# A planned order of five engines: a port rule in the planner, products ahead of the first load, and shifted leads

## The chip, the cores and the metric

One core of a Trainium2 chip runs the whole program. The metric is the time of one execution on the device, in microseconds (us), lower being better. Five engines work side by side, each through its own queue in order: TensorE (PE, matrix products into PSUM), VectorE (DVE), ScalarE (ACT), GpSimd (POOL) and SyncE (SP, which issues the DMAs). TensorE's clock is granted at one of two levels, 1.2 and 2.4 GHz; the profile gives it as a share of the higher one.

## What is computed

Linear attention over 8 batches, 8 heads, 576 tokens and 64 columns a head, with an RMS norm, then two layers over the 4608 tokens.

```python
kv = einsum('bhsd,bhse->bhde', k, v)
out = einsum('bhsd,bhde->bhse', q, kv)
x = out / sqrt(mean(out * out, -1) + 1e-6) * g_norm      # 4608 tokens x 512

h = x @ w_in                                             # 512 -> 2048
x = (h * cos(h)) @ w_out                                 # 2048 -> 512

h = x @ w2_in                                            # 512 -> 1024
s = h * softmax(h)
x = (s - mean(s)) / sqrt(var(s) + 1e-6) * g_ln @ w2_out  # 1024 -> 512
```

## The kernel before

Every product is done in three (`mm3`, L184 to L187): both operands are held as a high and a low part of a fast type, and high x high, high x low and low x high are added up in PSUM. A **split** makes the parts: ScalarE casts the high part (L427), and VectorE or GpSimd subtracts it to give the low part (L428). Layer one has 2048 hidden columns; the first quarter of them is computed straight (**phase 0**), the other three by a scheme with seven products in place of eight on 2 x 2 blocks (**phase 1**, blocks of 3 or 4 pairs of tiles, `first_h` and `first_out`); layer two uses the scheme too (**phase 2**, 18 pairs of tiles).

*Phase 0* goes with the attention. Token blocks m = 0 to 8 of 512 tokens each have four steps c = 0 to 3. A step has a product of four groups of three (`step_h`) into bank ps0 or ps1, the cosine chain on it (`cosine`: ScalarE L775, VectorE L777, ScalarE L780, VectorE L784, ScalarE L786, VectorE L788), and a product of four groups (`step_out`) into ps2 to ps5, put after the next step's `step_h`. After the fourth step ScalarE copies ps2 to ps5 out (`block_out`, L823), and the next block's first product needs these banks. In between stand the attention's tiles: k and v products (L528) and their copies (L589, L549), the product with q (L596, L646), a square (L600, L655), a reduction (L602, L657), GpSimd's power (L572, L573), a norm (L607, L673), a transposition (L612, L678) and the split of the result (L616, L618, L755, L757). The last block's four halves are taken from SBUF in `pair_prep` (four L427, then four L428). The weights come as 64-bit floats: a conversion is one ScalarE step (L399) and five others (L401, L403, L406, L408 on VectorE, L410 on VectorE at the start and on GpSimd later); jobs that convert the weights of the later phases run beside the steps of phase 0.

*Phase 1* begins with `prep_first`: a pair of tiles is loaded from DRAM, GpSimd makes four sums (L716), and four splits give the operands `rxa` and `rxb`.

The order of all instructions is written by a planner, `Flow.run`, before the program is built. Each operation is a task with an engine, a duration, its reads and writes, and a number `at`. The planner gives the engine that can start first its next task: among the tasks that can start by then, the one with the lowest `at`. So durations and `at` decide the order, and the engines then run it as far as data allow. A task with `port` is one of VectorE or GpSimd on SBUF. Where two such overlapped, the later one was lengthened by a share `PORT` of the overlap:

```python
a, b = port.get("DVE" if eng == "POOL" else "POOL", (0.0, 0.0))
t.end += PORT * max(0.0, min(b, t.end) - max(a, s))
```

Of the kernel before, what the change touches and what calls it, by code (L numbers as in the profile page):

```python
# [1393 lines left out]
```

## Time and profile before

| | |
|---|---|
| time of the kernel, median of 3 runs | 1261.39 us (1260.58 to 1262.4) |
| the profiled execution | 1262.73 us |
| its span, first to last instruction | 1260.9 us |
| busy: TensorE / VectorE / ScalarE / GpSimd | 1228.7 / 970.1 / 728.5 / 739.3 us |
| share of the span | 97% / 77% / 58% / 59% |
| share of the critical chain on TensorE | 91% |
| mean granted TensorE clock | 0.995 |

Matmuls are pipelined: a busy TensorE is not one at its peak, and the product shows as longer (0.39 us) than the distance from one to the next. An idle time in brackets is that of the engine just before the instruction, with what ended it. Tile names are the program's without numbers: `ps` is a PSUM bank, `rg` and `rx` hold operands, `fconv`, `pa` and `ws` belong to the conversions, `att` to the attention.

### The profile page before, as it was taken

Reading aid. Unit: us, or ns where it says so; the run is one execution under the profiler, and the core shown is the slowest. Engines: PE = TensorE matmul, PEld = TensorE weight load, DVE = VectorE, ACT = ScalarE, POOL = GpSimd, SP = SyncE. Lnnn points to the kernel's source line nnn. Section 1 sums busy time; section 2 is a strip of 40 time slices with the busy share of each in tenths; the row PEclk is TensorE's granted clock in tenths of the full one; section 3 lists DMA queues with packets and bytes.
Section 4 is the critical chain, followed back from the end, with each engine's and each line's share of the span. In section 5 each row is a group of like instructions: output and inputs, shape, how many; then the busy total and the mean of one; then the engine's idle time right before and its main releaser. Section 6 shows DMA issues by size and latency. Waiting matters only on the chain.

```text
span 1260.9 us, 20503 instructions
## 1 busy us (share of the span) xinstructions
PE 1228.7 (97%) x7224; PEld 1078.9 (86%) x7224; DVE 970.1 (77%) x1537; ACT 728.5 (58%) x1366; POOL 739.3 (59%) x686
## 2 busy tenths in 40 slices
PE   6899999988999999999999999999999999999998
PEld 4788887876999999888888888888898999898997
DVE  7977787887887887979685846654887888887875
ACT  5767666665663663656364625442666566666653
POOL 2355666666566667665773524262776667686732
PEclk9999999998999999999999999999999999999999
DMA  9799898686967958773866374499112121111000
GB/s 329 262 309 317 288 316 307 207 267 220 297 215 227 303 205 254 247 250 105 282 198 208 100 216 129 132 307 285 59 37 65 35 67 35 60 43 59 18 34 35
DMA packets 188009, 231.01 MB, mean 183 GB/s; under 512 B 11777, under 2 KB 123393, under 8 KB 187905
## 3 DMA queue, kind: packets, MB, share of 16 engines
q1 hardware_dynamic: 187904, 229.69, 56.0%
q8 instruction: 57, 0.93, 0.3%
q14 instruction: 48, 0.39, 0.1%
HBM read 159.91 MB, written 69.73 MB: 182 GB/s over the span
## 4 chain that ended last, share of the span: by engine, by line
PE 91%; DVE 5%; ACT 2%; issue 1%; DMA 0%; POOL 0%; DVEq 0%; ACTq 0%
PE ps L185 28%; PE ps L187 28%; PE ps L186 28%; PE ps L1043 2%; PE ps L646 2%; PE ps L528 2%; PE ps L678 1%; DVE fconv L403 0%; DVE rxb L428 0%; DVE fconv L401 0%; DMA fconv<-w 0%; DVE fconv L406 0%; DVE rxa L428 0%; ACT xf L684 0%; DVE fconv L408 0%
## 5 line engine op out<-in xcount | busy, mean ns | idle before, releaser
L185 PE MATMUL ps<-rg,rwo 128*128 128x512 f32 (+2 forms) x912 | 316.9, 347 | 5.5 <-ACT fh L823 4.1
L187 PE MATMUL ps<-rg,rwo 128*128 128x512 f32 (+2 forms) x912 | 314.0, 344 | 0.0
L186 PE MATMUL ps<-rg,rwo 128*128 128x512 f32 (+2 forms) x912 | 313.8, 344 | 0.0
L791 POOL TENSOR_TENSOR rg<-fh,rg 128x512 fp32r<-128x512 f32 (+1 forms) x120 | 151.5, 1274 | 160.1 <-ACT rg L786 153.2
L185 PEld LDWEIGHTS ps<-rg,rwo 128*128 128x128 f32 x912 | 172.4, 189 | 24.6 <-ACT fh L823 4.5
L186 PEld LDWEIGHTS ps<-rg,rwo 128*128 128x128 f32 x912 | 172.5, 189 | 17.8
L187 PEld LDWEIGHTS ps<-rg,rwo 128*128 128x128 f32 x912 | 172.2, 189 | 17.2
L185 PE MATMUL ps<-rxa,rwi 128*128 128x512 f32 (+1 forms) x384 | 146.7, 382 | 0.4 <-DVE fh L872 0.4
L186 PE MATMUL ps<-rxa,rwi 128*128 128x512 f32 (+1 forms) x384 | 144.5, 376 | 0.0
L187 PE MATMUL ps<-rxa,rwi 128*128 128x512 f32 (+1 forms) x384 | 144.3, 376 | 0.0
L775 ACT ACTIVATE fh<-ps 128x512 int32<-128x512 f32 (+1 forms) x126 | 71.5, 568 | 103.7 <-PE ps L187 92.1
L780 ACT ACTIVATE fh<-fh,const 128x512 f32<-128x512 f32 (+1 forms) x156 | 106.5, 692 | 36.3 <-DVE fh L777 35.5
L428 POOL TENSOR_TENSOR ws<-fconv,ws 128x512 fp32r<-128x512 f32 x68 | 87.4, 1288 | 42.3 <-ACT ws L427 27.1
L185 PE MATMUL ps<-rxb,rwi 128*128 128x512 f32 (+1 forms) x288 | 109.8, 381 | 0.0
L186 PE MATMUL ps<-rxb,rwi 128*128 128x512 f32 (+1 forms) x288 | 108.5, 377 | 0.0
L187 PE MATMUL ps<-rxb,rwi 128*128 128x512 f32 (+1 forms) x288 | 108.2, 376 | 0.0
L777 DVE SCALAR_TENSOR_TENSOR fh<-ps,fh 128x512 f32<-128x512 f32 (+1 forms) x126 | 80.9, 647 | 31.9 <-ACT fh L775 30.5
L923 DVE TENSOR_TENSOR mid<-ps,mid 128x512 f32<-128x512 f32 (+1 forms) x90 | 57.0, 634 | 60.0 <-PE ps L187 59.6
L410 POOL TENSOR_TENSOR fconv<-fconv 128x512 f32<-128x512 f32 x40 | 52.3, 1308 | 61.7 <-DVE fconv L408 61.7
L428 POOL TENSOR_TENSOR rwi<-sf,rwi 128x512 fp32r<-128x512 f32 x36 | 49.1, 1364 | 67.0 <-ACT rwi L427 66.9
L786 ACT CAST rg<-fh 128x512 fp32r<-128x512 f32 (+1 forms) x120 | 68.1, 577 | 29.7 <-DVE fh L784 28.4
L185 PEld LDWEIGHTS ps<-rxa,rwi 128*128 128x128 f32 x384 | 72.2, 188 | 11.4 <-DVE fh L872 0.7
(154 smaller groups left out, 2971.5 us busy)
## 6 DMA issues: line engine op xcount, KB each, us to landing
rwi<-wid SPq DMA_DIRECT2D x66, 512.0 KB, 5.1
rwo<-wod SPq DMA_DIRECT2D x88, 256.0 KB, 4.0
att<-qkv SPq DMA_DIRECT2D x32, 512.0 KB, 6.6
fconv<-w SPq DMA_DIRECT2D x28, 512.0 KB, 5.1
px<-fh SPq DMA_DIRECT2D x42, 256.0 KB, 4.4
xd<-xf SPq DMA_DIRECT2D x18, 512.0 KB, 4.4
wid<-ws SPq DMA_DIRECT2D x18, 512.0 KB, 3.9
xf<-xd SPq DMA_DIRECT2D x18, 512.0 KB, 4.9
```

The lines of the kernel that those rows point to most:

```text
L185: PE.matmul(ps, lhsT=lh, rhs=rh, start=start, stop=False, skip_group_check=more)
L186: PE.matmul(ps, lhsT=lh, rhs=rl, start=False, stop=False, skip_group_check=more)
L187: PE.matmul(ps, lhsT=ll, rhs=rh, start=False, stop=stop, skip_group_check=more)
L410: either(on_dve, 512, lambda eng: eng.tensor_tensor(out=buf[wk], in0=buf[yk], in1=buf[wk], op=ALU.add), r=[yk, wk], w=[wk], at=at)
L428: either(on_dve, n, lambda eng: eng.tensor_tensor(out=lo(), in0=src(), in1=f(hi()), op=ALU.subtract), [*keys, *hk], lk, at)
L528: PE.matmul(buf[bk][e * D:(e + 1) * D, p % 2 * D:(p % 2 + 1) * D], lhsT=k_[:, at_:at_ + D], rhs=k_[:, v_ + at_:v_ + at_ + D], start=(c == ...
L775: add("ACT", e_(0.6, 0.385, n), lambda: ACT.activation(out=tt().bitcast(I32), in_=h(), func=AF.Copy, scale=INV_2PI, bias=0.25), r=r, w=[tk ...
L777: add("DVE", e_(0.69, 0.418, n), lambda: DVE.scalar_tensor_tensor(out=tt(), in0=h(), scalar=INV_2PI, in1=tt().bitcast(I32), op0=ALU.mult, ...
L780: add("ACT", e_(0.725, 0.509, n), lambda: ACT.activation(out=tt(), in_=tt(), func=AF.Sin, bias=buf["halfpi"][:, 0:1], scale=TWO_PI), r=[tk ...
L786: add("ACT", e_(0.62, 0.405, n), lambda: ACT.copy(out=hi(), in_=g()), r=gk, w=hk, at=t + 2)
L791: either(on_dve, n, lambda eng: eng.tensor_tensor(out=lo(), in0=g(), in1=f(hi()), op=ALU.subtract), [*gk, *hk], lk, t + 2)
L923: add("DVE", e_(0.69, 0.418, n), lambda ak=ak, bk=bk: DVE.tensor_tensor(out=buf[ak][:, 0:n], in0=buf[bk][:, 0:n], in1=buf[ak][:, 0:n], op= ...
```

## The change

1. **The planner's port rule.** The lengthening by `PORT` is gone. A task with `port` now starts no sooner than the end of the other engine's last such task, less `LEAD` = 0.14 us. Three small operations of layer two (L1010, L1018) no longer count as `port`. `SLACK` of VectorE and GpSimd goes from 1.11 and 1.1 to 1.04.
2. **Products of the identity.** `N_WARM` = 15 products of the 128x128 identity with itself, into ps0, stand first on TensorE. Nothing reads them.
3. **Low parts of the first block of phase 1.** `prep_first` gives the fourth split (256 columns) of the first block's three pairs to GpSimd; before, all were VectorE's.
4. **Leads.** `at` values of jobs, loads, attention slots and of the softmax are shifted. `JOBS_LATE` and `COS_LEAD` are 0, `PAIR_DVE` is 2 and `FIRST_LEAD` 30, which changes nothing.

```diff
-E2_LEAD, SOFT_AT, SOFT_D, Q_OFF, CP_D = 15.86, 9.73, 0.94, 4.97, 10
+E2_LEAD, SOFT_AT, SOFT_D, Q_OFF, CP_D = 15.86, 10.63, -0.65, 4.97, 10
-PREP_LEAD, PREP_D, H_LATE, H_EARLY, JOB_AT = 4.22, 4, 0.41, 0.09, 8.99
+PREP_LEAD, PREP_D, H_LATE, H_EARLY, JOB_AT = 4.22, 4, 0.31, -0.01, 8.99
-SLOTS0, SLOT_T, SLOT_D, ... = 2, -7.89, 0.78, ...
+SLOTS0, SLOT_T, SLOT_D, ... = 2, -8.17, 0.14, ...
-CV_AHEAD, W_LOAD = 14.87, (-26.91, -24.38, -8.84, 7.59, 19.93, 10.16, 24.12, 28.58)
+CV_AHEAD, W_LOAD = 14.87, (-21.63, -23.98, -8.29, 7.59, 19.93, 10.16, 24.81, 28.58)
+N_WARM, JOBS_LATE, LATE_AT, LATE_D, FIRST_LEAD, COS_LEAD, FIRST_DVE, PAIR_DVE = 15, 0, 2.31, 9, 30, 0, 3, 2
-GAP, PE_LAT, PORT = 0.04, 0.18, 0.58
-SLACK = {"DVE": 1.11, "ACT": 1.1, "POOL": 1.1}
+GAP, PE_LAT, LEAD = 0.04, 0.18, 0.14
+SLACK = {"DVE": 1.04, "ACT": 1.1, "POOL": 1.04}
-ATT_LEAD, CV_LEAD, Q_LEAD, PRI = 8, 7.69, 16, 20
+ATT_LEAD, CV_LEAD, Q_LEAD, PRI = 7.15, 7.69, 16, 22.66
...
         def start(t):
-            return max(self.free.get(t.eng, 0.0), t.ready)
+            s = max(self.free.get(t.eng, 0.0), t.ready)
+            return max(s, locked["DVE" if t.eng == "POOL" else "POOL"] - LEAD) if t.port else s
...
             if t.port:
-                a, b = port.get("DVE" if eng == "POOL" else "POOL", (0.0, 0.0))
-                t.end += PORT * max(0.0, min(b, t.end) - max(a, s))
-                port[eng] = s, t.end
+                locked[eng] = t.end
...
+    for _ in range(N_WARM):
+        add("PE", 0.222, lambda: PE.matmul(buf[BANKS[0]][:, 0:P], lhsT=buf["ident"], rhs=buf["ident"], start=True,
+                                           stop=True), r=["ident"], w=[BANKS[0]], at=-50)
...
-    prep_first(item["t0"] // 2 + j, j, at - (PREP_LEAD if n else 30) + PREP_D * j, lambda i: True)
+    prep_first(item["t0"] // 2 + j, j, at - (PREP_LEAD if n else FIRST_LEAD) + PREP_D * j, lambda i: n or i < FIRST_DVE)
```

The engines' instructions are the same ones but for these; their order changes nearly everywhere. On TensorE, the last transposition of the attention (L678) stood nine groups of three ahead of the first product of the last block, and now stands 18 ahead; counted from the start, the last attention tiles come up to 13 groups earlier.

ScalarE at the start, before (`fconv` and `pa` hold two weight chunks in conversion, `rg_4` and `rg_5` are their high parts, `att_17` is the block of k-v products):

```order
L399 ACTIVATE fconv_0_101<-fconv_0_101 128x512
L399 ACTIVATE pa_8_127<-fconv_0_101 128x512
L427 CAST rg_4_89<-fconv_0_101 128x512
L589 COPY att_17_152<-ps2_0_175 64x64 x4
L600 ACTIVATE fh_0_115<-ps4_0_183 128x512
L427 CAST rg_5_90<-fconv_0_101 128x512
```
and in the new order:

```order
L399 ACTIVATE pa_8_127<-fconv_0_101 128x512
L399 ACTIVATE fconv_0_101<-fconv_0_101 128x512
L589 COPY att_17_152<-ps2_0_175 64x64 x2
L427 CAST rg_4_89<-fconv_0_101 128x512
L589 COPY att_17_152<-ps2_0_175 64x64 x2
L427 CAST rg_5_90<-fconv_0_101 128x512
L600 ACTIVATE fh_0_115<-ps4_0_183 128x512
```
The first product's copy now goes ahead of the first cast, and both casts ahead of the first square (L600).

VectorE in the change from phase 0 to phase 1 (`rxa`, `rxb` are operands of phase 1, `ps0` and `ps1` hold the steps of the last block), before:

```order
L428 TENSOR_TENSOR rxb_0_2588<-xf_0_110,rxb_0_2588 128x2x128
L401 TENSOR_SCALAR fconv_0_101<-fconv_0_101 128x512
L403 SCALAR_TENSOR_TENSOR fconv_0_101<-fconv_0_101 128x512
L428 TENSOR_TENSOR rxb_0_2588<-xf_1_111,rxb_0_2588 128x4x128
L428 TENSOR_TENSOR rxb_0_2588<-xf_1_111,rxb_0_2588 128x2x128
L777 SCALAR_TENSOR_TENSOR fh_0_115<-ps1_0_171,fh_0_115 128x512
L777 SCALAR_TENSOR_TENSOR fh_0_115<-ps0_0_167,fh_0_115 128x512
L784 TENSOR_TENSOR ps1_0_171<-ps1_0_171,fh_0_115 128x512
L784 TENSOR_TENSOR ps0_0_167<-ps0_0_167,fh_0_115 128x512
L788 TENSOR_TENSOR rg_1_86<-ps1_0_171,rg_1_86 128x512
L788 TENSOR_TENSOR rg_0_85<-ps0_0_167,rg_0_85 128x512
```
and in the new order:

```order
L401 TENSOR_SCALAR fconv_0_101<-fconv_0_101 128x512
L403 SCALAR_TENSOR_TENSOR fconv_0_101<-fconv_0_101 128x512
L777 SCALAR_TENSOR_TENSOR fh_0_115<-ps1_0_171,fh_0_115 128x512
L406 TENSOR_SCALAR fconv_0_101<-fconv_0_101 128x512
L784 TENSOR_TENSOR ps1_0_171<-ps1_0_171,fh_0_115 128x512
L408 SCALAR_TENSOR_TENSOR fconv_0_101<-fconv_0_101 128x512
L788 TENSOR_TENSOR rg_1_86<-ps1_0_171,rg_1_86 128x512
L428 TENSOR_TENSOR rxa_1_81<-sf_0_105,rxa_1_81 128x4x128
L777 SCALAR_TENSOR_TENSOR fh_0_115<-ps0_0_167,fh_0_115 128x512
L428 TENSOR_TENSOR rxb_0_2541<-xf_1_111,rxb_0_2541 128x4x128
L784 TENSOR_TENSOR ps0_0_167<-ps0_0_167,fh_0_115 128x512
```
The two L777, which stood one behind the other behind a conversion and two splits, stand apart, each soon followed by its own L784.

ScalarE in the same place, before (`ps2` to `ps5` are the banks that `block_out` empties):

```order
L823 COPY fh_0_115<-ps4_0_183 128x512
L399 ACTIVATE fconv_0_101<-fconv_0_101 128x512
L427 CAST rxb_0_2588<-xf_1_111 128x4x128
L427 CAST rxb_0_2588<-xf_1_111 128x2x128
L427 CAST ws_1_97<-fconv_0_101 128x512
L775 ACTIVATE fh_0_115<-ps0_0_167 128x512
L427 CAST ws_0_96<-fconv_0_101 128x512
L780 ACTIVATE fh_0_115<-fh_0_115,const_1_67 128x512
L823 COPY fh_0_115<-ps5_0_187 128x512
L780 ACTIVATE fh_0_115<-fh_0_115,const_1_67 128x512
```
and in the new order:

```order
L775 ACTIVATE fh_0_115<-ps1_0_171 128x512
L427 CAST rxa_0_80<-sf_1_106 128x4x128
L823 COPY fh_0_115<-ps2_0_175 128x512
L780 ACTIVATE fh_0_115<-fh_0_115,const_1_67 128x512
L823 COPY fh_0_115<-ps3_0_179 128x512
L823 COPY fh_0_115<-ps4_0_183 128x512
L786 CAST rg_1_86<-ps1_0_171 128x512
L427 CAST rxa_1_81<-sf_1_106 128x4x128
L775 ACTIVATE fh_0_115<-ps0_0_167 128x512
L780 ACTIVATE fh_0_115<-fh_0_115,const_1_67 128x512
L399 ACTIVATE fconv_0_101<-fconv_0_101 128x512
L823 COPY fh_0_115<-ps5_0_187 128x512
```
The copy of `ps5` had a conversion step (L399), four casts, one L775 and one L780 between it and that of `ps4`; now it has one L786, one cast, one L775, one L780 and one L399. Some 10 us earlier, where the last block's halves are split, the four casts stood behind all four copies of the block before, and stand now ahead of three of them.

## Rows read from the trace of the kernel before

**Rows 1.** Busy us (instructions) per stretch: PE, PEld, DVE, ACT, POOL; clock; DMA; GB/s.

```profile
0.00:60.00 60.00, 44.41 (x429) 36.02 (x430) 48.82 (x88) 36.11 (x73) 17.61 (x22) 1.00 0.88 291
60.00:260.00 200.00, 198.08 (x1368) 164.40 (x1367) 153.66 (x237) 135.43 (x251) 127.44 (x120) 1.00 0.86 288
260.00:320.00 60.00, 51.27 (x221) 41.90 (x220) 49.44 (x64) 35.18 (x65) 39.75 (x37) 0.91 0.80 254
320.00:1240.00 920.00, 919.57 (x5096) 822.58 (x5095) 709.13 (x1134) 515.38 (x967) 548.39 (x503) 1.00 0.47 152
...
sum 1261.00, PE 1228.66 PEld 1078.91 DVE 970.10 ACT 728.54 POOL 739.33; mean PE 245.73 PEld 215.78 DVE 194.02 ACT 145.71 POOL 147.87
```

**Rows 2.** Timeline of TensorE at the start: start us, us, engine, line, tiles, [idle before].

```profile
7.59 1.34 PE L528 MATMUL ps<-att 128*64 128x64 f32 x20 [7.59 <-DMA att<-qkv]
...
10.76 2.08 PE L596 MATMUL ps<-att,att 128*128 128x128 f32 x8
...
13.82 1.16 PE L596 MATMUL ps<-att,att 128*128 128x128 f32 x8
14.91 0.80 PE L528 MATMUL ps<-att 128*64 128x64 f32 x20
```

**Rows 3.** Timeline of the other engines at the start.

```profile
1.00 0.29 POOL masks.py:199 TENSOR_SCALAR_AFFINE_SELECT const<-const 128x128 f32<-128x128 f32 x1
...
5.36 0.43 DVE L401 TENSOR_SCALAR fconv<-fconv 128x512 uint32<-128x512 uint32 x1 [2.11 <-ACT fconv L399]
...
11.19 0.69 DVE L410 TENSOR_TENSOR fconv<-pa,fconv 128x512 f32<-128x512 f32 x1
...
12.87 0.60 ACT L600 ACTIVATE fh<-ps 128x512 f32<-128x512 f32 x1 [1.58 <-PE ps L596]
```

**Rows 4.** Waits of TensorE from 265 to 320: us, times, longest.

```profile
PE ps L185 <- ACT fh L823: 4.1, 1, 4.1
PE ps L185 <- DVE rg L788: 3.1, 2, 2.1
PE ps L186 <- DVE rg L428: 1.2, 1, 1.2
PE ps L185 <- DVE fh L872: 0.4, 1, 0.4
```

**Rows 5.** Timeline about the split of the last block's halves.

```profile
264.78 1.29 POOL L410 TENSOR_TENSOR fconv<-fconv 128x512 f32<-128x512 f32 x1
...
266.79 0.60 PE L678 MATMUL ps<-const,att 128*128 128x128 f32 x4
...
268.02 2.17 ACT L427 CAST rg<-xf 128x512 fp32r<-128x512 f32 x4
...
270.22 4.67 DVE L428 TENSOR_TENSOR rg<-xf,rg 128x512 fp32r<-128x512 f32 x4
...
270.38 1.67 POOL L410 TENSOR_TENSOR fconv<-fconv 128x512 f32<-128x512 f32 x1 [2.28 <-DVE fconv L408]
...
272.78 1.56 POOL L428 TENSOR_TENSOR ws<-fconv,ws 128x512 fp32r<-128x512 f32 x1 [0.73 <-ACT ws L427]
```

**Rows 6.** Busy us per stretch, as in rows 1, in the change of phases.

```profile
290.00:295.00 5.00, 1.88 (x9) 1.23 (x7) 5.00 (x5) 1.30 (x3) 4.90 (x5) 1.00 0.28 106
...
300.00:305.00 5.00, 5.00 (x16) 3.92 (x15) 0.91 (x2) 1.29 (x3) 0.49 (x1) 0.63 0.72 233
305.00:310.00 5.00, 5.00 (x23) 4.13 (x22) 4.02 (x7) 3.27 (x7) 3.33 (x4) 1.00 0.82 256
```

**Rows 7.** Timeline of VectorE and ScalarE in the change of phases.

```profile
289.90 1.67 DVE L403 SCALAR_TENSOR_TENSOR fconv<-fconv 128x512 uint32<-128x512 uint32 x1
...
291.49 2.62 DVE L428 TENSOR_TENSOR rxb<-xf,rxb 128x512 fp32r<-128x512 f32 x2
...
294.74 0.72 ACT L780 ACTIVATE fh<-fh,const 128x512 f32<-128x512 f32 x1 [3.70 <-DVE fh L777]
...
304.70 0.68 DVE L428 TENSOR_TENSOR rxa<-sf,rxa 128x512 fp32r<-128x512 f32 x1
```

More of the change, by code (lines that the diff above doesn't have):

```diff
@@ L48 @@
 BLOCKS = (0, 3), (6, 3), (12, 4), (20, 4), (28, 4)
-E2_LEAD, SOFT_AT, SOFT_D, Q_OFF, CP_D = 15.86, 9.73, 0.94, 4.97, 10
+E2_LEAD, SOFT_AT, SOFT_D, Q_OFF, CP_D = 15.86, 10.63, -0.65, 4.97, 10
 E2_JOBS = (0, 0, 0, 0, 0, 0, 1, 2, 0, 1, 2, 0, 1, 1, 0)
-PREP_LEAD, PREP_D, H_LATE, H_EARLY, JOB_AT = 4.22, 4, 0.41, 0.09, 8.99
+PREP_LEAD, PREP_D, H_LATE, H_EARLY, JOB_AT = 4.22, 4, 0.31, -0.01, 8.99
 T0, STEP_A, ITEM = 25, 8.14, 44.22
-SLOTS0, SLOT_T, SLOT_D, SLOT_LATE, SLOT_RATE, JOB0, JOB1 = 2, -7.89, 0.78, -10.82, 2.42, 5, 32
-CV_AHEAD, W_LOAD = 14.87, (-26.91, -24.38, -8.84, 7.59, 19.93, 10.16, 24.12, 28.58)
+SLOTS0, SLOT_T, SLOT_D, SLOT_LATE, SLOT_RATE, JOB0, JOB1 = 2, -8.17, 0.14, -10.82, 2.42, 5, 32
+CV_AHEAD, W_LOAD = 14.87, (-21.63, -23.98, -8.29, 7.59, 19.93, 10.16, 24.81, 28.58)
 MM4, MM2 = 0.68, 0.355
-GAP, PE_LAT, PORT = 0.04, 0.18, 0.58
-SLACK = {"DVE": 1.11, "ACT": 1.1, "POOL": 1.1}
-DMA_ISSUE, DMA_START, DMA_END, DMA_AHEAD = 0.5, 2.29, 1.84, 4
+N_WARM, JOBS_LATE, LATE_AT, LATE_D, FIRST_LEAD, COS_LEAD, FIRST_DVE, PAIR_DVE = 15, 0, 2.31, 9, 30, 0, 3, 2
+GAP, PE_LAT, LEAD = 0.04, 0.18, 0.14
+SLACK = {"DVE": 1.04, "ACT": 1.1, "POOL": 1.04}
+DMA_ISSUE, DMA_START, DMA_END, DMA_AHEAD = 0.5, 2.1, 1.84, 4
 OVER = {"DVE": 0.084, "ACT": 0.104, "POOL": 0.042}
 XPRI = 10
-ATT_LEAD, CV_LEAD, Q_LEAD, PRI = 8, 7.69, 16, 20
-KV_T = 0.59
-PAIR_C, TR_LAG, OUT_LAG = 21.19, 19.02, 29.5
+ATT_LEAD, CV_LEAD, Q_LEAD, PRI = 7.15, 7.69, 16, 22.66
+KV_T = 0.64
+PAIR_C, TR_LAG, OUT_LAG = 20.75, 19.02, 29.5
 SMALL = ("nmx", "z", "sp", "nmp", "v", "zz", "ry")
@@ L126, in run @@
     def run(self):
-        ready, port, served = {}, {}, 0.0
+        ready, locked, served = {}, {"DVE": -1e3, "POOL": -1e3}, 0.0
         def release(t):
@@ L767, in pair_prep @@
                   lambda col=col: xo(m, 0)[:, :, col], lambda col=col: xo(m, 1)[:, :, col],
-                  [("xhk", i, j, h)], [("xlk", i, j, h)], at, True)
+                  [("xhk", i, j, h)], [("xlk", i, j, h)], at, h < PAIR_DVE)
     def cosine(h, psrc, tk, n, hi, lo, r, hk, lk, t, on_dve, there=False):
@@ L806, in step_h @@
         cosine(lambda: buf[hb], True, tts(), 512, lambda: rg(j)[:, 0, :], lambda: rg(j)[:, 1, :],
-               [hb], [("gs", j)], [("gsl", j)], at, True, True)
+               [hb], [("gs", j)], [("gsl", j)], at - COS_LEAD, True, True)
     def step_out(c, j, at):
@@ L1010, in soft @@
         add("DVE", 1.216, lambda: DVE.tensor_reduce(out=sm("nmx"), in_=buf[hk], axis=AX.X, op=ALU.max, negate=True),
-            r=[*halves], w=[("nmx", n)], at=at)
+            r=[*halves], w=[("nmx", n)], at=at, ps=True)
         add("ACT", 1.24, lambda: ACT.activation(out=buf[ek], in_=buf[hk], func=AF.Exp, bias=sm("nmx")[:, 0:1],
@@ L1018, in soft @@
         add("DVE", 0.15, lambda: DVE.tensor_scalar(out=sm("nmp"), in0=sm("sp"), scalar1=-1.0 / FP, scalar2=None,
-                                                  op0=ALU.mult), r=[("sp", n)], w=[("nmp", n)], at=at)
+                                                  op0=ALU.mult), r=[("sp", n)], w=[("nmp", n)], at=at, ps=True)
         add("ACT", 0.2, lambda: ACT.activation(out=sm("zz"), in_=sm("z"), func=AF.Square, scale=1e-3,
@@ L1225, in tile_kernel @@
     jobs = [x for fp in range(2, NFP) for x in (job_in(fp), job_out(fp, 0), job_out(fp, 1))]
+    late, jobs = jobs[len(jobs) - JOBS_LATE:], jobs[:len(jobs) - JOBS_LATE]
     n_jobs = len(jobs)
@@ L1278, in half_out @@
             first_out(item, half, at, dur / KC)
+    for i, job in enumerate(late):
+        job(T1_ + LATE_AT + LATE_D * i)
     prev = None
```

## The prediction

> **What bounds the kernel now.** I read the busy time by stretch first [rows 1]. TensorE is busy 1228.66 of 1261 us, so the order of the other engines can matter only where TensorE stands still. In the 920 us from 320 to 1240 it stands still 0.43 us, in the 200 us from 60 to 260 1.92 us: nothing is to be had there. It stands still 15.59 us in the first 60 us (7.59 of them before the first product, whose k and v have not landed [rows 2]), 8.73 us from 260 to 320, and what is left, 5.67 us, at the end. Then I read the waits of the 60 us about the change of layers [rows 4]: 4.1 + 3.1 + 1.2 + 0.4 = 8.8 us, all of TensorE, for ScalarE's copies (L823) and for VectorE. Idle time there is paid twice: from 300 to 305 the granted clock is 0.63 (that is the 1.2 GHz level for most of it), and 5 us hold 16 products in place of 23 [rows 6]. At 5/23 = 0.22 us each (0.65 a group of three) that is 7 x 0.22 = 1.5 us lost. There is a second such stretch after the 3.1 us for L788; with the parts on either side I put both at 3.5 us. So the change of layers costs 8.8 + 3.5 = 12.3 us, the start 8.0 beyond the landing of k.
>
> Why VectorE is late there: it is busy for all of the 5 us from 290 to 295, in which TensorE does 1.88 us [rows 6]. Four L428 take 4.67 us [rows 5]; one takes 0.68 where GpSimd is idle [rows 7], so 4 x 0.68 = 2.72 would do. GpSimd's own two instructions took 1.67 and 1.56 us in that time, against 1.29 before it [rows 5]. Later an L403 takes 1.67 and two L428 take 2.62 [rows 7]. **That is the collision the new planner lays out for**, and in the old order one such pile (L403, two L428) stands ahead of two L777. L780 waits 3.70 us for L777 [rows 7], L823 stands behind L780, and TensorE's product waits 4.1 us for the bank that L823 empties [rows 4].
>
> The Trainium skill bears on this, in "SBUF — State Buffer", Who interferes with whom: a VectorE instruction with two SBUF inputs and a GpSimd instruction that reads SBUF take one port in turn, and the later one blocks wholly. The trace agrees only nearly: alone the six instructions of [rows 5] come to 2.72 + 2.58 = 5.30 us, and they were done in 4.67.
>
> **The change, part by part. (1) The start.** Fifteen products of the identity run before k lands. Four 128x128 products show as eight passes [rows 2], so fifteen are 30; at 2.08/8 = 0.26 to 1.16/8 = 0.145 us each they take 4.4 to 7.8 us. The identity is written at 1.29 [rows 3], so they end between 5.7 and 9.1 and cost between nothing and 1.5 us of the first k pair at 7.59. I take nothing: in the trace the passes went from 0.26 to 0.145 us some 6 us after TensorE's first work, and here that should fall inside the 30. What they give: the first two k-v groups and the first q group go from 1.34, 1.34 and 2.08 to 0.80, 0.80 and 1.16 [rows 2], 2.0 us of TensorE. Little of it reaches the path, since the new ScalarE order puts both weight casts (L427) ahead of the first L600, and the second of them needs ten VectorE conversion steps. These ran from 5.36 to 11.19 + 0.69 = 11.88, with one L428 among them that is now behind them, so they end near 11.3 [rows 3]. A copy and a cast then bring L600 to about 12.2 against 12.87 [rows 3]: 0.7 us. On VectorE the third norm (L607) has one reduction (L602) less ahead of it: another 0.6. A little more (0.2) for smaller moves makes 1.5 us; ends 0 and 4 us (half of the 8.0).
>
> **(2) The change of layers.** What goes. The products on the last block's first tiles waited 1.2 us for the splits L428 of its halves. The last transposition (L678) began at 266.79 and the last split ended at 270.22 + 4.67 = 274.89 [rows 5]: 8.1 us. The old order gives nine groups of three to fill them (5.9 us), the new one 18 (11.7 us): gone. The 3.1 us for L788: the old order has L777 behind the four splits and L784 behind four conversion steps, the new one has L777 and L784 of that step ahead of the splits: gone. The 4.1 us: in the new order the L777 that the L780 ahead of the last bank's copy waits for has one L428 straight ahead of it, where it had a conversion and two L428: gone. With the waits the half clock goes, 3.5 us. What comes. (a) On ScalarE the four casts (2.17 us [rows 5]) now stand ahead of three of the four bank copies of the block before. From the last L678 to the end of the third copy are L678, the copy out of its bank, four casts, and five more of 0.54 to 0.72 (the four casts' share, and L780 [rows 7]): 0.6 + 0.7 + 2.2 + 3.0 = 6.5, while TensorE has eight groups (5.2 us) to do. That is a new wait of 1.3; ends 0.5 (starts overlap) and 2.7 (the cast between them waits for one GpSimd instruction of 1.29). I take 1.5. (b) VectorE. Between the first split of the last block and the split of the third tile of layer one there are 41 instructions in the new order, 34 of 0.69 and seven of 0.43 (L401, L406) [rows 3]: 26.5 us. TensorE covers them with 54 groups (35.1 us) less some 3.5 until the first split: 31.6. That leaves 5.1 us for collisions. The stretched instructions of [rows 5, 7] cost 4.67 - 2.72, 1.67 - 0.69 and 2.62 - 1.36, together 4.2 us, in 9 us of some 30 of VectorE's work; the rest is less dense, and I put the whole at 7.5. With as many TensorE waits 2.4, and with a third fewer nothing; three splits of 256 columns move from VectorE to GpSimd, which lengthens GpSimd's share. I take 2.5, ends 0 and 8. Sum: -12.3 + 1.5 + 2.5 = -8.3.
>
> By the skill's rule of turns alone, GpSimd's work in that stretch (nine of 1.29 and 19 half as wide) and VectorE's 18 two-input instructions could not lie side by side: 11.6 + 12.3 + 12.4 = 36.3 against 35.1, so 1.2 us more of waiting would come, and 1253.8 in place of the time below.
>
> **(3) What pays for it.** The last attention tiles come earlier, the last by 13 groups (8.5 us), into a stretch where VectorE and ScalarE already work; TensorE waits there 1.9 us in 200 [rows 1]. I take +1.0, ends 0 (DMA and engines have room: VectorE 153.7, ScalarE 135.4 of 200) and +6.
>
> **(4) The rest.** Layer one after 320 and the whole of layer two: TensorE has 0.43 us to lose or gain; the reordering hides behind it. If a new order let it wait as in 60 to 260 it would cost 0.4 to 3; I take 0. The end: TensorE's last 120 instructions stand in the same order; the last L1092 and L1012 swap, which is 0.4 us either way. I take 0.
>
> Sum: -1.5 - 8.3 + 1.0 = **-8.8 us**. The profiled execution took 1262.73 us, 1.83 over its span of 1260.9, and lies 1.34 above the median; so 1253.9 for it, and **1252.6** against the median of 1261.39.
>
> **Rivals.** A, *no change*: VectorE stays the bound of the change of layers. It does the same instructions but three, collisions come to their 7.5 us wherever they stand, a wait for L788 or L823 forms again and the clock falls again. For it: VectorE is busy 49.44 of 60 us there [rows 1]. Against it: the longest wait was one pile ahead of one L777, and the new order has none. Then (2) is -2 and the time 1259.4 or more, up to 1263.
>
> B, *slower*: the attention tiles that were pulled forward. Each half tile needs a reduction, GpSimd's power, a norm, a transposition and a split in turn, and all of these now share VectorE with steps that TensorE waits for. The nearest row is the wait for L823, 4.1 us [rows 4]. Two such waits and a half-clock stretch after each (1.5 to 2) come to 12 us and more than eat the 9.8 us won elsewhere; the case turns slower from 12.3 us of new waits on. 1264 to 1268.
>
> C, *the identity's products do not carry*: they end early, the clock falls again before k lands, and the start keeps its rates. The trace has the pattern (TensorE does 1.88 of the 5 us from 290, and soon after the granted clock is 0.63 [rows 6]). That takes 0.7 from (1): 1253.3, inside the forecast's range. The Trainium skill has the rule behind it in "TensorE: Matmul & The Clock Gate", Part 1: the slow state is the default, activity lifts it, idleness brings it back; the trace's 2.08 and then 1.16 us for the same eight passes agree.
>
> **How the numbers follow.** Changes of this kernel within 0.2% (2.5 us) can't be told from none. The forecast (with C) has 0.76, A 0.13, B 0.11. The range takes the forecast's own spread, from -14 (start 4, the change of layers 10) to -3, and reaches into A until two in ten are left out: 1247.0 to 1261.0. Faster 0.76, same 0.13, slower 0.11.
>
> **What would show it.** TensorE: idle from 260 to 320 falls from 8.73 to about 4 and its clock stays at 1.00 there; no wait of over 2 us for L823 or L788. The 1.2 us before the last block's products is gone, a wait for L823 of about 1.5 us stands some 10 us earlier. At the start L596's first eight passes take about 1.2 us, and the first L600 starts near 12.2. VectorE's L428 in the change of layers take nearer 0.7 each. I am wrong if TensorE's idle time between 60 and 260 grows beyond 5 us, if a stretch at half clock is left between 260 and 320, or if waits appear between 320 and 1240.

## The result

| | before | after |
|---|---|---|
| time, median | 1261.41 us (1260.58 to 1262.4) | 1248.40 us (1248.34 to 1248.95) |
| span of the profiled execution | 1260.9 us | 1246.5 us |
| busy: TensorE / VectorE / ScalarE / GpSimd | 1228.7 / 970.1 / 728.5 / 739.3 us | 1229.8 / 938.1 / 728.2 / 740.7 us |

The ratio is 0.9898, with a 95% interval of 0.988 to 0.9915: 13.0 us faster by the medians, 14.4 by the two profiled spans; the profiled execution of the kernel before is one of its longer ones, 1.3 us above the median. 8.8 were forecast; the time lies inside the range, 1.4 us above its lower end.

The page of the kernel after, its table of engines' busy time and its line of the granted clock:

```profile
PE 1229.8 (99%) x7254; PEld 1079.8 (87%) x7254; DVE 938.1 (75%) x1534; ACT 728.2 (58%) x1366; POOL 740.7 (59%) x689
...
PEclk9999999999999999999999999999999999999999
```

The busy time by stretch (columns as in [rows 1]):

```profile
0.00:60.00 60.00, 50.71 (x473) 41.05 (x474) 51.56 (x92) 37.97 (x76) 18.02 (x24) 1.00 0.91 312
60.00:260.00 200.00, 199.63 (x1380) 166.16 (x1380) 152.40 (x239) 139.10 (x258) 131.87 (x123) 1.00 0.87 292
260.00:320.00 60.00, 59.47 (x293) 52.41 (x293) 51.10 (x77) 39.16 (x76) 47.17 (x45) 1.00 0.93 306
320.00:1240.00 920.00, 916.86 (x5087) 817.23 (x5086) 681.75 (x1126) 512.02 (x958) 543.68 (x498) 1.00 0.46 147
```

The last of these stretches holds the last 14 us of the changed program too, which lie behind 1240 in the kernel before: of the 3.1 us in which TensorE stands still there, 1.8 are two waits at the very end. From 260 to 320 TensorE stands still 0.53 us in place of 8.73, at a clock of 1.00 in place of 0.91, and does 293 products in place of 221. Its waits from 255 to 330 are two, where [rows 4] had five over 8.8 us (columns as there):

```profile
PE ps L185 <- DVE rg L788: 0.4, 1, 0.4
PE ps L185 <- ACT fh L823: 0.2, 1, 0.2
```

The start, where [rows 2] and [rows 3] answer (TensorE, then ScalarE's first square):

```profile
1.34 5.01 PE L1133 MATMUL ps<-const 128*128 128x128 f32 x30 [1.34 <-POOL const masks.py:199]
7.20 0.80 PE L528 MATMUL ps<-att 128*64 128x64 f32 x20 [0.84 <-DMA att<-qkv]
8.97 0.80 PE L528 MATMUL ps<-att 128*64 128x64 f32 x20 [0.97 <-DMA att<-qkv]
9.87 1.13 PE L596 MATMUL ps<-att,att 128*128 128x128 f32 x8
```

```profile
12.21 0.60 ACT L600 ACTIVATE fh<-ps 128x512 f32<-128x512 f32 x1
```

Stretches of equal time hold different work in the two kernels. So I also compared them at points of TensorE's order at which both have the same products behind them (the identity's left out). The times at these points are read from the two traces; the differences are worked out from them.

| point of TensorE's order | before | after | difference | gained since the point above |
|---|---|---|---|---|
| row 82, first block | 42.56 | 39.67 | -2.89 | 2.9 |
| row 985, ahead of the last block's first product | 268.84 | 264.55 | -4.28 | 1.4 |
| row 1101, layer one begins | 308.89 | 291.51 | -17.38 | **13.1** |
| row 3946, in the change to layer two | 895.75 | 878.50 | -17.26 | -0.1 |
| row 6150, last products | 1256.95 | 1242.64 | -14.30 | **-3.0** |

So there are three stories: the start and the attention, the change of phases, which gave more than forecast, and layer two, which gave 3 us back.

### The profile page after: what moved, and what is told of

It reads as the page before. It is cut to its first block, busy times and chain, and to the rows that moved or that the text cites. A ratio compares the mean times of both kernels' runs of the same rounds, so it can differ in the third digit from the quotient of the medians.

```text
span 1246.5 us, 20559 instructions
## 1 busy us (share of the span) xinstructions
PE 1229.8 (99%) x7254; PEld 1079.8 (87%) x7254; DVE 938.1 (75%) x1534; ACT 728.2 (58%) x1366; POOL 740.7 (59%) x689
## 4 chain that ended last, share of the span: by engine, by line
PE 92%; DVE 4%; ACT 2%; issue 1%; POOL 1%; DMA 0%; DVEq 0%; ACTq 0%; POOLq 0%
PE ps L185 28%; PE ps L187 28%; PE ps L186 28%; PE ps L646 2%; PE ps L1043 2%; PE ps L528 1%; DVE fconv L1052 1%; PE ps L678 1%; ACT e2r L1066 0%; POOL att L573 0%; DMA fconv<-w 0%; ACT fconv L1055 0%; ACT rg L427 0%; ACT xf L684 0%; DVE fh L777 0%
## 5 line engine op out<-in xcount | busy, mean ns | idle before, releaser
L780 ACT ACTIVATE fh<-fh,const 128x512 f32<-128x512 f32 (+1 forms) x156 | 104.9, 689 | 44.7 <-DVE fh L777 43.2
L775 ACT ACTIVATE fh<-ps 128x512 int32<-128x512 f32 (+1 forms) x126 | 71.1, 568 | 87.2 <-PE ps L187 68.0
L428 POOL TENSOR_TENSOR ws<-fconv,ws 128x512 fp32r<-128x512 f32 x68 | 86.7, 1280 | 48.6 <-ACT ws L427 28.0
L777 DVE SCALAR_TENSOR_TENSOR fh<-ps,fh 128x512 f32<-128x512 f32 (+1 forms) x126 | 80.9, 648 | 26.1 <-ACT fh L775 24.6
L786 ACT CAST rg<-fh 128x512 fp32r<-128x512 f32 (+1 forms) x120 | 67.4, 576 | 29.0 <-DVE fh L784 28.2
L185 PEld LDWEIGHTS ps<-rxa,rwi 128*128 128x128 f32 x384 | 72.1, 188 | 12.5 <-DVE fh L979 1.6
L187 PEld LDWEIGHTS ps<-rxa,rwi 128*128 128x128 f32 x384 | 72.1, 188 | 11.5
```

The costliest lines, as they stand in the source:

```text
L185: PE.matmul(ps, lhsT=lh, rhs=rh, start=start, stop=False, skip_group_check=more)
L187: PE.matmul(ps, lhsT=ll, rhs=rh, start=False, stop=stop, skip_group_check=more)
L428: either(on_dve, n, lambda eng: eng.tensor_tensor(out=lo(), in0=src(), in1=f(hi()), op=ALU.subtract), [*keys, *hk], lk, at)
L775: add("ACT", e_(0.6, 0.385, n), lambda: ACT.activation(out=tt().bitcast(I32), in_=h(), func=AF.Copy, scale=INV_2PI, bias=0.25), r=r, w=[tk ...
L777: add("DVE", e_(0.69, 0.418, n), lambda: DVE.scalar_tensor_tensor(out=tt(), in0=h(), scalar=INV_2PI, in1=tt().bitcast(I32), op0=ALU.mult, ...
L780: add("ACT", e_(0.725, 0.509, n), lambda: ACT.activation(out=tt(), in_=tt(), func=AF.Sin, bias=buf["halfpi"][:, 0:1], scale=TWO_PI), r=[tk ...
```

## The experiments

"The change" below is the changed kernel. What a run won in a stretch is worked out at the same points of the order, against the kernel named. Two things about the change have to be set right first. The operations of layer two that no longer count as `port` are two in each softmax, not three. And three more constants of the planner moved: `PAIR_C` (the pitch of layer two's pairs of tiles) from 21.19 to 20.75, `KV_T` from 0.59 to 0.64 and `DMA_START` from 2.29 to 2.1.

### The identity's products, taken out of the change and put alone into the kernel before (e1, e2)

```diff
-N_WARM, ... = 15, ...
+N_WARM, ... = 0, ...
```

> The changed kernel without the 15 products of the identity; every engine's order is otherwise the same. In the changed kernel TensorE reaches its 83rd row (end of the first block's second step) 2.9 us sooner than before. Theory A (the products carry the start: TensorE's first passes run at the higher rate): most of it goes, 1250.4 to 1251.4 us against 1248.4. Theory B (the new ScalarE and VectorE order carries it, as the prediction put it, 1.5 us, and the faster passes reach no path): 1248.4 to 1249.4.

> The kernel before with the 15 products of the identity alone put ahead; its order is otherwise untouched. Theory A: 1.5 to 3 us less, 1258.5 to 1260. Theory B: within 0.7 us of 1261.4. If the two do not add up (this one gains nothing, the run without them loses 2 us), the products pay only where the weight casts come early.

Measured: e1 1249.47 us (1248.91 to 1250.51), 1.1 above the change by the medians; by the traces it loses 1.36 us up to row 82 and never gains it back (1.32 at the end). TensorE at the start of e1:

```profile
7.38 1.34 PE L528 MATMUL ps<-att 128*64 128x64 f32 x20 [7.38 <-DMA att<-qkv]
9.24 1.33 PE L528 MATMUL ps<-att 128*64 128x64 f32 x20 [0.53 <-ACT att L589]
10.51 2.08 PE L596 MATMUL ps<-att,att 128*128 128x128 f32 x8
```

These passes are slow again, 1.34 and 2.08 us as in [rows 2], where the change has 0.80 and 1.13. The first square (L600) starts at 12.62 in e1 against 12.21 in the change and 12.87 in the kernel before:

```profile
12.62 0.60 ACT L600 ACTIVATE fh<-ps 128x512 f32<-128x512 f32 x1 [0.27 <-PE ps L596]
```

e2 took 1260.28 us (1258.81 to 1262.99), ratio 0.9989 (0.9979 to 0.9999), 1.4 below before. By the traces 0.44 us are won up to row 82 and 2.4 in the change of phases, where e2's order is that of the kernel before. The waits there are not shorter; the two longest in e2 (one line up, L824 is L823), where [rows 4] have 4.1 and 3.1:

```profile
PE ps L186 <- ACT fh L824: 4.8, 1, 4.8
PE ps L186 <- DVE rg L789: 2.4, 2, 2.1
```

What differs is the clock after the wait of 2.1 us for L788. From 280 to 285, first the kernel before, then e2 (columns as in [rows 1]):

```profile
280.00:285.00 5.00, 5.00 (x16) 3.97 (x17) 4.83 (x7) 2.81 (x6) 3.32 (x3) 0.68 0.91 338
280.00:285.00 5.00, 5.00 (x24) 4.10 (x23) 4.83 (x7) 4.16 (x9) 3.77 (x3) 1.00 0.87 308
```

These 2.4 us, then, are not shown to be the identity's: the kernel before itself was seen from 1260.0 to 1262.84, its 17 executions with a mean granted clock of 0.997 from 1260.0 to 1261.96, its seven with 0.995 from 1262.39 up.

What follows: theory A holds for the change (1.3 us), though e1's and e2's times each lie between the two forecasts. The new ScalarE order and the rest are worth the other 1.5 us of the start (e3, with the new order and no identity, gains 1.66 up to row 82). Without the early casts the products pay a third of that.

### The port rule alone, and the change without it (e3, e9)

e3 is the kernel before with the new rule and its SLACK; e9 is the change with the old ones. Rule and SLACK were not tried apart, so "the rule" below is both. The diff of e3 (e9's is its reverse):

```diff
-            return max(self.free.get(t.eng, 0.0), t.ready)
+            s = max(self.free.get(t.eng, 0.0), t.ready)
+            return max(s, locked["DVE" if t.eng == "POOL" else "POOL"] - LEAD) if t.port else s
...
-SLACK = {"DVE": 1.11, "ACT": 1.1, "POOL": 1.1}
+SLACK = {"DVE": 1.04, "ACT": 1.1, "POOL": 1.04}
```

> The kernel before with the planner's new port rule (LEAD 0.14, SLACK 1.04) and nothing else of the change. In the changed kernel the change of phases (last block to the first tiles of layer one) took 13.1 us less. Theory P (the rule does it, by setting VectorE's and GpSimd's work apart): 10 to 14 us of that come here, 1248 to 1252, with no wait over 1 us for L823 or L788 between 260 and 320. Theory L (the leads do it: 18 groups ahead of the last block's first product in place of nine): the wait for the halves' splits (1.2 us) and most of the idle time stay, 1257 to 1262.

> The changed kernel with the old port rule and the old SLACK; identity products, leads and the splits given to GpSimd stay. Theory P (the rule makes the gain in the change of phases; the leads alone do not): the start keeps its 1.4 us of the identity, layer two takes 3 us less than in the changed kernel, and the change of phases loses 6 us or more of its 13: 1252 to 1259 us. Theory L (the leads and the three splits make the gain): 1245 to 1249.

Measured: e3 1263.38 us (1262.76 to 1264.3), ratio 1.0015 (1.0006 to 1.0025); e9 1267.78 us (1266.5 to 1271.75), ratio 1.0055 (1.0037 to 1.0074). Each half alone makes the kernel slower, by 1.7 and 6.5 us against the runs of the kernel before beside it; both together make it 13 us faster. By stretch, in us won (+) or lost (-) against before (at the nearest rows that the orders share, 1089 and 3902 among them):

| stretch | change | e3, rule alone | e9, the rest alone |
|---|---|---|---|
| to row 82 | +2.9 | +1.7 | +1.9 |
| to row 985 | +1.4 | +2.2 | -3.5 |
| change of phases | +13.1 | +8.9 | +6.7 |
| layer one | -0.1 | -2.1 | -6.0 |
| layer two | -3.0 | -11.6 | -4.6 |

Part of e9's 3.5 us is the clock: it was granted at 0.52 from 45 to 52 us, behind two waits of 4.3 us in all. TensorE's waits in e3, first from 260 to 310, then from 905 to the end (one row down in line numbers: L787 is L788, L992 is L993, L1030 is L1031):

```profile
PE ps L184 <- DVE rg L787: 3.0, 1, 3.0
```

```profile
PE ps L184 <- ACT fconv L992: 3.0, 4, 1.0
PE ps L1042 <- DVE fconv L1030: 3.0, 2, 1.5
PE ps L184 <- ACT fh L1091: 1.2, 1, 1.2
```

and in e9 from 260 to 330 (one line up):

```profile
PE ps L186 <- DVE rg L789: 5.2, 2, 4.9
PE ps L186 <- DVE fh L785: 1.6, 1, 1.6
```

In e3 the waits for L823, L428 and one of those for L788 are gone, and the one wait left is 3.0 us for L788, ahead of the last block's first product. In e9 the same wait is 4.9 us. Both times lie above both of their forecasts. Theory P is right for the change of phases in kind (8.9 of 13.1); e3's total is spoiled by what neither theory named: layer two pays 11.6 us for the rule. That e9 is slower than the kernel before shows that the shifted leads do not fit the order of the old rule.

The wait of 3.0 us is also what e3 lacks against the change in this stretch. Up to there e3 is 0.4 us behind the change; the change waits 0.4 us at the same product; and the products behind e3's wait come at the low level:

```profile
270.00:275.00 5.00, 5.00 (x15) 3.96 (x16) 2.51 (x5) 1.28 (x3) 4.99 (x5) 0.66 1.11 362
```

Wait and clock make 2.6 and 1.6 us, together the 4.2 between 8.9 and 13.1.

### Layer two: the softmax lead, the flags, the old rule there (e4, e10, e11, e5)

```diff
-E2_LEAD, SOFT_AT, SOFT_D, ... = 15.86, 10.63, -0.65, ...
+E2_LEAD, SOFT_AT, SOFT_D, ... = 15.86, 9.73, 0.94, ...
```

> The changed kernel with SOFT_AT and SOFT_D as before (9.73, 0.94): the order differs only in layer two. There the changed kernel gave back 3.0 us of what it had won, in some 13 short waits of the first product of a pair of tiles for the bank that L979 (VectorE) empties. Theory S (the shifted softmax lead makes them): 1245.4 to 1246.4 us. Theory R (the new port rule makes them, whatever the lead): 1247.9 to 1249.

e4 took 1249.88 us (1249.13 to 1250.63), 1.5 above the change and against both forecasts: under the new rule the new lead is the better one, so it is not what makes the loss.

e10 adds to e3 the flags of the change, and e11 its softmax lead and pair pitch too:

```diff
...
-            r=[*halves], w=[("nmx", n)], at=at)
+            r=[*halves], w=[("nmx", n)], at=at, ps=True)
...
-                                                  op0=ALU.mult), r=[("sp", n)], w=[("nmp", n)], at=at)
+                                                  op0=ALU.mult), r=[("sp", n)], w=[("nmp", n)], at=at, ps=True)
...
-PAIR_C, TR_LAG, OUT_LAG = 21.19, 19.02, 29.5
+PAIR_C, TR_LAG, OUT_LAG = 20.75, 19.02, 29.5
```

> The kernel before with the new port rule and with the two small operations of each softmax (L1010, L1018) taken out of the port, as the change has them. With the rule alone layer two lost 12 us. Theory F (the flags mend most of it, since under the rule every small operation waits for GpSimd's last in the plan): 7 us or more come back, 1253.5 to 1256.5. Theory G (the softmax lead and the pitch mend it): 1261 to 1264.

> As the run before, and with the new softmax lead and pair pitch: from row 4000 on TensorE's order is nearly that of the changed kernel. With the 11.2 us that the rule alone won up to layer two and some 3 us given back there: 1252.5 to 1254.5 us, whichever of flags and lead mends the rest. If layer two still loses over 5 us, the other leads (loads, low parts) are what mends it.

e10 took 1256.28 us (1254.93 to 1256.98), e11 1253.53 (1252.92 to 1254.7), both as theory F and the sum had it. Layer two's loss goes from 11.6 us (rule alone) to 4.7 (flags) to 2.5 (softmax lead and pitch), near the 3.0 of the change. So the flags on two operations are worth 7 us, and the softmax lead and pitch 2. L1010 is not small: it reduces 1024 columns, in 1.21 to 1.22 us in each of its 36 executions in either kernel. In each, 32 of the 36 lie beside work of GpSimd, whose 512-column instructions there take their usual 1.30 us. So the traces show no collision of the two, and a rule that makes L1010 take turns models a conflict that isn't there in these traces.

What is left of it in the change is spread thin. TensorE's waits in the change from 889 us to the end name L979, which empties a bank for the next pair of tiles, three times, and a timeline shows one of these places (VectorE, then TensorE):

```profile
PE ps L185 <- DVE fh L979: 0.6, 3, 0.2
```

```profile
974.91 1.48 DVE L979 TENSOR_TENSOR fh<-ps,fh 128x512 f32<-128x512 f32 x2
...
975.65 0.50 PE L185 MATMUL ps<-rxa,rwi 128*128 128x512 f32 x1 [0.21 <-DVE fh L979]
```

I counted the distances from one product's start to the next: from the first tiles of layer two on, 16 of the 256-column products are followed late in the change (by 0.05 to 0.37 us), one in the kernel before; eleven of the 16 stand ahead of a 512-column product as in the rows above. Together they are 2.6 us late, most of the 3.0, though the wait list shows only 0.6.

The last run lays out layer two by the old rule and all else by the new one:

```diff
-            return max(s, locked[...] - LEAD) if t.port else s
+            return max(s, locked[...] - LEAD) if t.port and t.at < NEW_TO else s
...
-            t.end = s + t.dur * SLACK.get(eng, 1.0)
+            t.end = s + t.dur * (SLACK if t.at < NEW_TO else SLACK_OLD).get(eng, 1.0)
```

> The changed kernel in which tasks with an at of 900 and more (the last block of layer one and layer two) are laid out by the old rule, with the old SLACK, softmax lead, pair pitch, DMA start and port flags: TensorE's order is that of the changed kernel in its first 3500 rows and that of the kernel before from row 4000 on. Theory R (the new rule costs 3.0 us in layer two, the earlier gain stays whole): 1245.0 to 1246.0 us. Theory K (the loss comes with the earlier start, whatever the order there): 1247.9 to 1248.9.

Measured: **1245.69 us** (1245.49 to 1245.99), ratio 0.9875 (0.9859 to 0.9892): 2.7 below the change, and faster than both kernels. Up to row 2997 it is 0.1 us off the change, at row 6150 2.8 ahead of it. Theory R has the time: the new layout of layer two costs 3 us, and the 17 us won before it are kept in full. The run puts back rule, SLACK, softmax lead, pitch, DMA start and flags at once; flags and lead lessen the loss under the rule (e4, e10, e11), which leaves the rule with its SLACK as the likely cost, but no run takes these apart.

### Parts of the change ahead of layer one (e6, e7)

```diff
-N_WARM, ..., FIRST_DVE, PAIR_DVE = 15, 0, 2.31, 9, 30, 0, 3, 2
+N_WARM, ..., FIRST_DVE, PAIR_DVE = 15, 0, 2.31, 9, 30, 0, 4, 2
```

> The changed kernel with FIRST_DVE = 4: all splits of the first block of phase 1 are VectorE's again. In the change of phases VectorE has some 41 instructions (26.5 us) and about 5 us of stretching, just what TensorE's work covers. Theory C (the cover is used up): three more splits of 0.43 us ahead of the layer cost 1 to 3 us, 1249.4 to 1251.4, with a wait for L788 or L823 of over 1 us. Theory N (there is room left): within 0.6 us of 1248.4.

```diff
-SLOTS0, SLOT_T, SLOT_D, ... = 2, -8.17, 0.14, ...
+SLOTS0, SLOT_T, SLOT_D, ... = 2, -7.89, 0.78, ...
```

> The changed kernel with SLOT_T and SLOT_D as before (-7.89, 0.78), so that the attention's last tiles come later (the last transposition 14 rows later on TensorE). Theory E (the early attention pays, by giving the splits of the last block's halves time): the 1.2 us wait for them comes back and the change of phases loses 1 to 4 us, 1249.4 to 1252.4. Theory F (it costs, as the prediction took it, 1.0 us): 1247 to 1248.2.

Measured: e6 1251.08 us (1250.76 to 1251.19), 2.7 above the change; e7 1252.70 us (1252.11 to 1254.18), 4.3 above. Both sizes are near those of the first theories, and both places are not. TensorE's waits from 255 to 330, first of e6, then of e7:

```profile
PE ps L185 <- DVE fh L784: 0.7, 1, 0.7
PE ps L185 <- ACT fh L884: 0.6, 1, 0.6
```

```profile
PE ps L185 <- DVE fh L784: 1.8, 2, 1.4
PE ps L185 <- DVE rg L788: 1.7, 1, 1.7
```

e6 is level with the change up to row 1101 (0.1 us) and loses 1.6 us in the first 200 rows of layer one, where a cosine chain of layer one (L784) ends late: the three splits move VectorE's load from the change of phases into the first tiles of layer one. e7 is 0.8 us behind at row 82, and it loses 1.3 us at row 1040, with a wait for L788 and none for the halves' splits, and 2.2 more in the first rows of layer one. Early attention pays, then, but not by the 1.2 us wait that I had it pay with. Between rows 82 and 985 e7 is 0.7 us quicker than the change, and so the early tiles cost at most that there.

### What a late VectorE costs (e8, e12)

One split of the change is repeated, STALL = 8 times in e8 and 4 in e12, in an order that is otherwise the same:

```diff
-        add("DVE" if on_dve else "POOL", dur, lambda: fn(eng), r=r, w=w, at=at)
+        add("DVE" if on_dve else "POOL", dur, lambda: [fn(eng) for _ in range(max(1, int(on_dve)))], r=r, w=w, at=at)
...
-    prep_first(..., lambda i: n or i < FIRST_DVE)
+    prep_first(..., lambda i, j=j, n=n: (1 + STALL * (n == 0 and j == 0 and i == 2)) if n or i < FIRST_DVE else 0)
```

> The changed kernel in which one split (L428) of the first block of phase 1, ahead of the L777 at 281 us, is done nine times in place of one; the order is else the same. That is 8 x 0.68 = 5.4 us more of VectorE. The next L788 that TensorE needs ends 1.4 us ahead of its use, and VectorE is idle 0.7 us on the way: a wait of TensorE of about 3.3 us near 288.8. Theory twice (idle time is paid again by a stretch at half clock): one of 2 to 4 us follows and the kernel loses 4.3 to 5.5 us, 1252.7 to 1253.9. Theory once: 3.0 to 3.8 us, 1251.4 to 1252.2. Theory none (later slack takes it up): under 1.5 us.

> As the stalled run (e8), but the split is done five times in place of one. In e8 nine took 9.10 us (1.09 alone in the changed kernel: 8.0 us more), TensorE waited 6.9 us for L823 and the kernel lost 9.2 us by its trace, so 2.3 us beyond the wait, with the granted clock at 0.91, 0.50 and 0.90 in the three stretches of 5 us from 285. Here 4 x 1.0 = 4.0 us more, so a wait of 2.9. Theory fixed (any such wait brings the half clock for about as long): 2.9 + 2.3 = 5.2 us lost, 1253.0 to 1254.2. Theory share (a third of the wait comes on top): 3.9 us, 1251.9 to 1252.8. Theory none (a short wait keeps the clock): 2.9 us, 1250.9 to 1251.6.

Measured: e8 1258.36 us (1257.35 to 1258.61), 10.0 above the change (9.2 by the traces); e12 1254.26 us (1253.63 to 1254.94), 5.9 above (5.2). VectorE's repeated split and the product that waits, in e8 (lines one up: L824 is L823):

```profile
280.32 9.10 DVE L429 TENSOR_TENSOR rxa<-sf,rxa 128x512 fp32r<-128x512 f32 x9
```

```profile
291.85 0.79 PE L186 MATMUL ps<-rg,rwo 128*128 128x512 f32 x1 [6.87 <-ACT fh L824]
292.44 0.63 PE L187 MATMUL ps<-rg,rwo 128*128 128x512 f32 x1
...
295.43 0.63 PE L188 MATMUL ps<-rg,rwo 128*128 128x512 f32 x1
295.85 0.46 PE L186 MATMUL ps<-rg,rwo 128*128 128x512 f32 x1
```

and busy time by stretch in e8 (columns as in [rows 1]):

```profile
285.00:290.00 5.00, 0.00 (x0) 0.00 (x0) 4.85 (x7) 0.00 (x0) 1.69 (x2) 0.91 0.06 25
290.00:295.00 5.00, 3.15 (x8) 2.48 (x8) 4.78 (x8) 3.04 (x6) 1.30 (x1) 0.50 0.45 136
295.00:300.00 5.00, 5.00 (x21) 4.08 (x20) 3.61 (x6) 3.66 (x7) 3.93 (x5) 0.90 0.52 170
```

In e12, the split, the busy time by stretch and the product that waits:

```profile
280.27 5.80 DVE L429 TENSOR_TENSOR rxa<-sf,rxa 128x512 fp32r<-128x512 f32 x5
```

```profile
285.00:290.00 5.00, 1.50 (x4) 1.21 (x5) 4.78 (x7) 2.26 (x4) 2.61 (x3) 0.81 0.19 65
290.00:295.00 5.00, 5.00 (x20) 4.09 (x19) 4.20 (x6) 3.83 (x7) 2.62 (x4) 0.85 0.71 228
```

```profile
288.50 0.80 PE L186 MATMUL ps<-rg,rwo 128*128 128x512 f32 x1 [3.62 <-ACT fh L824]
289.10 0.63 PE L187 MATMUL ps<-rg,rwo 128*128 128x512 f32 x1
...
291.60 0.39 PE L187 MATMUL ps<-rg,rwo 128*128 128x512 f32 x1
```

In the change the split took 1.09 us, so e8 adds 8.0 us and e12 4.7; TensorE waits 6.9 and 3.6. The margin of that chain (L777, L780, L823) is thus 1.1 us in both. Beyond the wait e8 loses 2.3 us and e12 1.6. This is the 1.2 GHz level: after the wait the products start 0.43 us apart (292.44 to 295.43 are eight products in 2.99 us) where 0.23 is usual, for some 4 us in e8 and 2.7 in e12. e12's 5.2 us are the sum of theory "fixed" (its median lies just above that range), but they came by a longer wait, 3.6 us and not 2.9: the 1.6 beyond it lie between the 2.3 of e8 and a third of the wait, 1.2, so the two runs don't decide between "fixed" and "share". Theory "none" is out. My forecast for e8 was short because nine splits took 1.01 us each, not 0.68, and because the wait came through L823, not L788.

## Why the prediction held, and where its sizes were off

**The start: 2.9 us, not 1.5.** The order's part was right in size: orders without the identity win 1.5 to 1.7 us (e1, e3). That L600 was forecast near 12.2 and starts at 12.21 is luck, though: without the identity it starts at 12.62 (e1), behind a wait for TensorE's L596, so the order alone brings 0.25 of the 0.7 us that the forecast gave it. The step that was mis-sized is the identity's, put at nothing ("little of it reaches the path"). It is worth 1.3 us (e1). [Rows 2] had the reason: from 10.76 to 14.91 TensorE's passes follow one another, so TensorE itself was on the path there, beside the conversion. The products of the identity were forecast to end between 5.7 and 9.1 and cost nothing; they end at 6.35, ahead of the first k product at 7.20. Rival C, that the clock falls again before k lands, is out: the first L528 takes 0.80. Its price of 0.7 us was one that (1) had put down to the order.

**The change of phases: 13.1 us, not 8.3.** Of the 12.3 us forecast to go, the waits went (8.8 down to 0.6 us). The half clock had been put at 3.5 us; what is left of the 13.1 after 8.2 us of waits is 4.9. Most of it can be counted: from the last attention tiles to the first tiles of layer one, 27 products of the kernel before start over 0.28 us after a 512-column product with no idle time between, 5.0 us late in all; six in the change, 0.7 us. e3, e8 and e12 show the same, 1.6 to 2.3 us behind a wait of 3.0 to 6.9. This part belongs to the execution that was profiled: e2, whose waits there are as long, has 14 such products and 2.4 us. The two new costs (1.5 and 2.5 us) did not come. (a) The chain of copies behind the four casts came as computed, 6.3 us from the last L678 to the product that needs the bank, but TensorE's eight groups and that L678 take 5.9, not 5.2, and the wait is 0.2 us. (b) The step that failed is the cover, the 54 groups at 0.65 us less 3.5 before the first split, 31.6 us. From the first split, at 255.44, to the product that needs the third tile's split, at 291.72, TensorE had 36.3 us: a group takes 0.68 us (three starts 0.227 apart), not the rounded 0.65, and the first split began 2.7 us after the last L678, not 3.5 after; that L678, small waits and the slower products behind them are the rest. VectorE's side was put too high as well, at 26.5 + 7.5 = 34.0 us: its instructions show 0.68 us and start 0.60 us apart.

```profile
270.15 0.69 DVE L788 TENSOR_TENSOR rg<-ps,rg 128x512 fp32r<-128x512 f32 x1
270.76 0.68 DVE L777 SCALAR_TENSOR_TENSOR fh<-ps,fh 128x512 f32<-128x512 f32 x1
271.36 0.68 DVE L408 SCALAR_TENSOR_TENSOR fconv<-fconv 128x512 f32<-128x512 uint32 x1
```

It was busy 32.4 of 36.2 us:

```profile
255.44:291.66 36.22, 35.53 (x154) 28.31 (x152) 32.42 (x45) 25.92 (x48) 29.26 (x26) 1.00 0.90 290
```

The 7.5 us put down for collisions were right: summing what each VectorE instruction takes beyond the 10th percentile of its line and shape gives 7.4 us from 253 to 292 in the change, and 9.3 from 257 to 306 in the kernel before. So the claim that VectorE's splits would take nearer 0.7 us each was wrong, and with it the reading that the rule wins there mainly by fewer collisions. The four splits of the halves stand beside GpSimd's work as before and take 4.69 us, where [rows 5] have 4.67:

```profile
L428 DVE TENSOR_TENSOR rg<-xf,rg 128x512 fp32r<-128x512 f32 x4 | 4.7, 1230 | 0.0
```

What changed is what stands behind them; that this order, and not the 2 us of collisions saved, carries the stretch is read from the waits that went and was not tried by itself. In the whole trace VectorE does get faster, 970.1 to 938.1 us busy, and in layer one that buys nothing, because TensorE was never waiting there. Rival A (collisions keep VectorE the bound) had the collisions right and the end wrong. Its time of 1259.4 counts the -2 alone; with the -1.5 and +1.0 of the forecast's sum it is 1258.9.

**The attention: 1.4 us won, not 1.0 lost.** TensorE's idle time between 60 and 260 fell from 1.92 to 0.37 us. The rule does it (2.2 us in e3), and the early tiles cost at most 0.7 (e7). Neither of the two waits of 4 us by which rival B was priced came.

**Layer two: 3.0 us lost, not 0.** This is the other step that failed. "The reordering hides behind it" took an idle time of 0.43 us as a sign of room; it was a sign of a fit. I had bounded the term by 0.4 to 3 us, and it came at the far end. The prediction's own sign of being wrong, waits between 320 and 1240, came true with the 0.6 us for L979. The planner's rule of turns, which helps where VectorE and GpSimd both work on SBUF, had cost 11.6 us here without the flags and the leads.

The two large errors (4.8 us in the change of phases, 3.0 in layer two) were of opposite sign; it is luck that the second took back part of the first. Which part of the change takes away the wait of 3.0 us for L788 that the rule alone leaves (e3; 3.5 us in e10, 3.4 in e11) is settled in part: the old slots (e7) bring 1.3 us of it back, the splits on GpSimd (e6) none. The other leads were not tried one by one.

By the rule of turns in the Trainium skill ("SBUF — State Buffer", Who interferes with whom) the prediction had 1.2 us more of waiting. No run here shows that wait; the four splits and GpSimd's two instructions beside them again overlapped in part, 4.69 us for what alone is put at 5.30. The sum for it set the 36.3 us against the whole cover of 35.1, where step (b) took 31.6.

## What to carry to other kernels

A planner's rule that models a real conflict better still has to be paid for where that conflict bounds nothing: give it a range of the program, and look at every stretch in which the bound engine had no idle time before, since there it can only lose. When work is to be hidden, count both sides from start to start, up to the instruction that needs the last result, because a rounding of 0.03 us in 54 groups, a start off by 0.8 us and durations that overlap by 0.08 us turned a margin into a wait. Before an operation is made to take turns, look in a trace whether it is ever stretched: L1010 was not. Two parts that were tuned together (a rule and the leads) can each be a loss alone, so undoing one of them doesn't tell its worth.

## What the runs showed of the hardware that was not expected

After a wait of TensorE of 3.6 us the products came at the 1.2 GHz level for 2.7 us, after one of 6.9 us for some 4 us; the loss beyond the wait was 1.6 and 2.3 us. After one of 1.7 us (e7) the granted clock stayed at 1.00. A wait of 2.1 us was followed by the low level in the profiled execution of the kernel before (0.68 from 280 to 285) and not in that of e2 (1.00), which differs from it only ahead of the first load. So the same order of instructions, run again, can cost some 2 us more or less with the same waits. The change, which has no long wait there, is also the steadier one: its four runs lie within 0.6 us, the four of the kernel before beside them within 1.8. That this is the clock's doing fits the clocks on record, and was not tried by itself.
